# Feature-major output for token chunks 0 to 2 of a linear-attention and MLP block, with a new order of the first transfers

## The chip, the cores and the metric

The kernel runs on one core of a Trainium2 chip. The metric is device time in microseconds. Before the change the median of 13 runs is 205.41 us, the lowest 205.16, the highest 206.95. A profile is one execution taken by the hardware profiler; its span goes from the first to the last instruction, and its own device time is a little more than its span.

The engines are TensorE (PE; its weight loads PEld), VectorE (DVE), ScalarE (ACT), GpSimd (POOL) and SyncE (SP). SP here issues most transfers, in the order of its queue, and waits at each for what the transfer needs; ScalarE issues a few. The 16 DMA engines move the data.

## The reference

For x of 2048 tokens and 640 features (bf16), with 32 heads of 20 features and an MLP of 1536:

```python
xn = _layernorm(x, axis=-1)
return x + _A_ref(xn, A_wqkv, A_wo) + _B_ref(xn, B_w1, B_b1, B_w2, B_b2)
# _A_ref: linear attention
phi = lambda t: jnp.where(t > 0, t + 1, jnp.exp(t)) + 1e-6
pq, pk = phi(q), phi(k)
kv = jnp.einsum("bhsd,bhse->bhde", pk, v)
z = jnp.einsum("bhsd->bhd", pk)
o = einsum("bhqd,bhde->bhqe", pq, kv) / (einsum("bhqd,bhd->bhq", pq, z)[..., None] + 1e-6)
# ... then o @ wo
# _B_ref: gelu(x @ w1 + b1) @ w2 + b2
```

## The kernel before

Tokens are cut into 16 tiles of 128 (NT) and 4 chunks of 512 (NC). Features are 5 blocks of 128 (DT), MLP features 12 blocks (JT). A small planner records every instruction on its engine's list in the order of the program text and works out the semaphore waits from what each reads and writes. So each engine's order is the program's order. PSUM's eight banks are handed out in a ring: `take(1)` gives the next bank, `take(2)` the next even pair.

The stages on TensorE, in order:

1. Start: some matmuls on zeros, then LayerNorm of token tiles 0 and 1, their transposes through TensorE (L352, L389), and the first products with W1 (`h_first`, L400). `h_first(0, ...)` does the first two of the five feature blocks for four output blocks (8 matmuls, needing W1's rows 0 to 255), then the other three (12 matmuls, needing rows 256 to 639), and has pieces of tile 1's transposes between.
2. H: `h_unit` (L368) makes GELU(xn W1 + b1), feature-major, into HG (features x tokens), in matmuls of up to 512 tokens. From tile 4 on, xn is turned to xnT by DMA transposes on SP (L473).
3. K: 160 matmuls (L508); the activation `phi` on ScalarE and VectorE writes phi(K) to PK, which lies in the buffer of x. VectorE then sums it over tokens (`token_sum`), and `z_step` turns that sum by two DMA transposes.
4. G: xn^T phi(K), 160 matmuls (L541).
5. Q: `q_chunk(c)` (L553) makes phi(Q), feature-major, into PQ, chunk by chunk; between the chunks `kvt_step` (L567) and `mt_block` (L585) make the matrix M = (masked K^T V) Wo, which five DMA transposes put into Msb (L593). `x_again` loads x a second time into its old buffer (L638).
6. Out: for every token tile, 24 matmuls of HG with W2 and 10 of PQ with Msb (L669), each with a 128x128 block of tokens as weights and 320 output features as moving columns: two PSUM banks a tile. `out_w2(t)` does the first 24, `out_fin(t, b)` the other 10, two tiles behind. VectorE then adds PSUM and x (x with b2 added before, `xb`, L642) to out_sb (L689), and SP stores it (L692). The last tile (`out_last`, L706) goes in three pieces.

Beside the out stage run the denominators of the attention, a chunk ahead: `den_part` (L599, L602; VectorE, five a chunk), `den_gather` (L613; DMA over partitions), `den_inv` (L618, L621; VectorE), `den_spread` (L627; DMA), and `rden_scale` (L633; VectorE), which multiplies PQ's five blocks of the chunk by 1/den and so must be done before that chunk's PQ matmuls. For chunks 1 to 3 gathers and spreads go half on SP and half on ScalarE.

The first transfers' issues, SP and ScalarE (`dma_x` L245, `dma_w` L249):

```python
dma_x(0, 1)
dma_w("scalar", b1tmp[:], B_b1.rearrange("(a p) -> a p", p=P), r_b1tmp)
dma_w("scalar", W1[:, 0:KA, 0:FW], w1v[:, 0:KA, 0:FW], r_W1A)
dma_x(1, 1)
dma_w("sync", W1[:, KA:DT, 0:FW], w1v[:, KA:DT, 0:FW], r_W1[0])
dma_w1(1)
dma_x(2, 1)
dma_w1(2)
```

W1 comes in three blocks of 512 columns (FW); the first in two parts, rows 0 to 255 (KA = 2) and 256 to 639. SP's queue so has x0, x1, rows 256 to 639, block 1, x2, block 2; ScalarE's has b1 and rows 0 to 255.

Of the kernel before, what the change touches and what calls it, by code (L numbers as in the profile page):

```python
# [5 lines left out]
ALU = AluOpType  # L6
ACT = mybir.ActivationFunctionType
P = 128
FP32 = mybir.dt.float32
# [103 lines left out]
def bass_parallel_sum__linear_attn_block__dense_activation_gelu__prompt_kernel(  # L113
# [4 lines left out]
    NT = S // P  # L118
# [19 lines left out]
    with contextlib.ExitStack() as es:  # L138
# [13 lines left out]
        GTb = W1f[:, 0:DT * D].rearrange("p (k d) -> p k d", k=DT)  # L152
        KVT = W1f[:, DT * D:DT * D + NG * GW].rearrange("p (g d) -> p g d", g=NG)
        MT = W1f[:, DT * D + NG * GW:DT * D + NG * GW + DT * D].rearrange("p (b d) -> p b d", b=DT)
        Wqkv = sb("Wqkv", [P, DT, 3 * D], BF16)
        W2 = sb("W2", [P, JT, D], BF16)
        Wo = sb("Wo", [P, NG, D], BF16)
# [3 lines left out]
        zhl = Mf[:, 2 * D:4 * D].rearrange("p (a d) -> p a d", a=2)  # L161
        b1tmp = sb("b1tmp", [JT, P], BF16)
        b1c = sb("b1c", [P, JT], FP32)
        b2bc = sb("b2bc", [P, D], BF16)
        ident = sb("ident", [P, P], BF16)
        maskKV = sb("maskKV", [P, GW], BF16)
# [25 lines left out]
        def take(n):  # L192
            b = ring[0]
            if n == 2 and b % 2:
                b += 1
            b %= 8
            ring[0] = (b + n) % 8
            return b

        def bank(b, lo=0, hi=512):  # L200
            return ps[:, b * 512 + lo: b * 512 + hi]
# [14 lines left out]
        r_W1 = [R_("W1_%d" % i) for i in range(NW1)]  # L216
        r_Wq, r_Wk, r_Wv, r_W2 = R_("Wq"), R_("Wk"), R_("Wv"), R_("W2")
        r_Wo = [R_("Wo%d" % i) for i in range(2)]
        r_b1tmp, r_b1c, r_b2 = R_("b1tmp"), R_("b1c"), R_("b2")
        r_ident, r_small, r_masks, r_warm = R_("ident"), R_("small"), R_("masks"), R_("warm")  # L220
        r_stats = [[R_("stats%d_%d" % (i, h)) for h in range(2)] for i in range(4)]
# [18 lines left out]
        xv = A_x.rearrange("b s d -> (b s) d")  # L240
        ov = out.rearrange("b s d -> (b s) d")

        def dma_x(t, n):
            src = xv[t * P:(t + n) * P, :].rearrange("(t p) d -> p t d", p=P)
            Pl.ins("sync", lambda e: e.dma_start(x_in[:, t:t + n, :], src),  # L245
                   writes=r_x[t:t + n], dma=True)

        def dma_w(eng, dst, src, res):
            Pl.ins(eng, lambda e: e.dma_start(dst, src), writes=[res], dma=True)  # L249
# [5 lines left out]
            dma_w(eng, W1[:, :, i * FW:(i + 1) * FW], w1v[:, :, i * FW:(i + 1) * FW], r_W1[i])  # L255
        KA = 2
        dma_x(0, 1)
        dma_w("scalar", b1tmp[:], B_b1.rearrange("(a p) -> a p", p=P), r_b1tmp)
        dma_w("scalar", W1[:, 0:KA, 0:FW], w1v[:, 0:KA, 0:FW], r_W1A)
        dma_x(1, 1)  # L260
        dma_w("sync", W1[:, KA:DT, 0:FW], w1v[:, KA:DT, 0:FW], r_W1[0])
        dma_w1(1)
        dma_x(2, 1)
        dma_w1(2)
# [219 lines left out]
        def phi(src, b, nb, dst, res_dst, extra_w):  # L484
# [3 lines left out]
            else:  # L488
# [10 lines left out]
                                                       op0=ALU.max, op1=ALU.add),  # L499
                   reads=br + [re], writes=[res_dst] + extra_w)  # L500

        ring_e = [0]
        for t in range(NT):
            b = take(2)
# [44 lines left out]
        def q_chunk(c, after=None):  # L549
            cc = slice(c * CW, (c + 1) * CW)  # L550
            for j in range(DT):
                b = take(1)
                Pl.ins("tensor", [(lambda e, k=k, j=j, b=b: e.matmul(  # L553
                    bank(b), Wqkv[:, k, j:D:DT], xnT[:, k, cc],
                    start=(k == 0), stop=(k == DT - 1))) for k in range(DT)],
                    reads=[r_Wq] + r_xnT[c * CH:(c + 1) * CH], writes=[B_[b]])
                phi(bank(b), b, 1, PQ[:, j, cc], r_PQ[c][j], [])
                if after:
                    after(j)
# [4 lines left out]
        def kvt_step():  # L564
            for gs in parts:
                b = take(1)
                Pl.ins("tensor", [(lambda e, k=k, i=i, b=b, g0=gs[0]: e.matmul(  # L567
                    bank(b, GW * (i - g0), GW * (i - g0) + gw[i])[0:GW, :],
                    Wqkv[:, k, 2 * D + ge[i]:2 * D + ge[i] + GW],
                    GTb[:, k, GW * i:GW * i + gw[i]], start=(k == 0), stop=(k == DT - 1)))  # L570
                    for i in gs for k in range(DT)], reads=[r_Wv] + r_GT, writes=[B_[b]])
                for lo, hi, w in ([(0, G1, GW)] if gs[0] == 0 else [(G1, NG - 1, GW), (NG - 1, NG, gw[-1])]):
                    n = hi - lo
                    src = bank(b, GW * (lo - gs[0]), GW * (lo - gs[0]) + n * w)[0:GW, :].rearrange("p (g d) -> p g d", g=n)
                    msk = maskKV[0:GW, GW * lo - ge[lo]:GW * lo - ge[lo] + w].unsqueeze(1).to_broadcast([GW, n, w])
                    Pl.ins(v, lambda e, lo=lo, hi=hi, w=w, src=src, msk=msk: e.tensor_tensor(
                        out=KVT[0:GW, lo:hi, 0:w], in0=src, in1=msk, op=ALU.mult),
                        reads=[B_[b], r_masks], writes=[r_KVT] + r_W1)
# [30 lines left out]
        def den_gather(c):  # L609
            for q in range(MH):  # L610
                dst = y4[c % 2][H * q:H * (q + 1)]
                src = yv[c % 2][:, SW * q:SW * (q + 1)]
                Pl.ins(dma_q(c, q), lambda e, dst=dst, src=src: e.dma_start(dst, src),  # L613
                       reads=[r_y[c % 2]], writes=[r_y4[c % 2][q]], dma=True)

        def den_inv(c):
            s = c % 2
            Pl.ins(v, lambda e: e.tensor_reduce(out=den_sb[:, s, :], in_=y4[c % 2].rearrange("p m s -> p s m"),  # L618
                                                axis=mybir.AxisListType.X, op=ALU.add),
                   reads=r_y4[c % 2], writes=[r_den[s]])  # L620
            Pl.ins(v, lambda e: e.reciprocal(rden[:, s, :], den_sb[:, s, :]), reads=[r_den[s]], writes=[r_rden[s]])  # L621
# [8 lines left out]
        def rden_scale(c):  # L630
            cc = slice(c * CW, (c + 1) * CW)
            for j in range(DT):
                Pl.ins(v, lambda e, j=j: e.tensor_tensor(out=PQ[:, j, cc], in0=PQ[:, j, cc], in1=rdv[c], op=ALU.mult),  # L633
                       reads=r_rdb[c] + [r_PQ[c][j]], writes=[r_PQ[c][j]])

        def x_again(c):
            src = xv[c * CW:(c + 1) * CW, :].rearrange("(t p) d -> p t d", p=P)
            Pl.ins("sync", lambda e: e.dma_start(x_res[:, c * CH:(c + 1) * CH, :], src),  # L638
                   writes=[r_xr[c]] + r_PK[c * CH:(c + 1) * CH], dma=True)

        def xb(t):
            Pl.ins(v, lambda e: e.tensor_tensor(out=x_res[:, t, :], in0=x_res[:, t, :], in1=b2bc[:], op=ALU.add),  # L642
                   reads=[r_xr[t // CH], r_b2], writes=[r_xb[t]])
# [2 lines left out]
            x_again(c)  # L646
        q_chunk(0)
        kvt_step()
        q_chunk(1)

        def mt_and_den(j):
# [5 lines left out]
        den_spread(0)  # L657

        stores = []
        out_l = sb("out_l", [P, D], BF16)  # L660
        r_outl = [R_("outl%d" % i) for i in range(3)]

        def mm_ops(t, i):
# [11 lines left out]
        def out_w2(t, lo=0, hi=JT, b=None):  # L675
            b = take(2) if b is None else b
            for i in range(lo, hi):
                Pl.ins("tensor", [mm(b, t, i, 0), mm(b, t, i, 1)], reads=mm_reads(t, i), writes=B_[b:b + 2],
                       mark=(i == JT - 1))
            return b  # L680

        def out_fin(t, b):
            s = t % 2
            for i in range(JT, JT + DT):
                Pl.ins("tensor", [mm(b, t, i, 0), mm(b, t, i, 1)], reads=mm_reads(t, i), writes=B_[b:b + 2],
                       mark=(i == JT + DT - 1))
            if t >= CH:
                xb(t)
            Pl.ins(v, lambda e: e.tensor_tensor(out=halves(out_sb[:, s, :]), in0=pair(b),  # L689
                                                in1=halves(x_res[:, t, :]), op=ALU.add),  # L690
                   reads=B_[b:b + 2] + [r_xb[t]], writes=[r_out[s]])
            stores.append(Pl.ins("sync", lambda e: e.dma_start(ov[t * P:(t + 1) * P, :], out_sb[:, s, :]),  # L692
                                 reads=[r_out[s]], dma=True))
# [21 lines left out]
        def den_parts(c, lo, hi):  # L715
            for j in range(lo, hi):
                den_part(c, j)

        bs = [out_w2(t) for t in range(4)]
        den_parts(1, 0, DT)  # L720
        den_gather(1)
        rden_scale(0)
        for t in range(CH):
            xb(t)
        den_inv(1)
        den_spread(1)
        den_parts(2, 0, 1)
        out_fin(0, bs[0])
        den_parts(2, 1, 2)
        out_fin(1, bs[1])  # L730
        rden_scale(1)
        for t in range(2, NT - 1):
            out_fin(t, bs[t])
            if t == 2:
                den_parts(2, 2, DT)
                den_gather(2)
            elif t == 4:
                den_inv(2)
                den_spread(2)
            elif t == 5:  # L740
                den_parts(3, 0, DT)
                den_gather(3)
            elif t == 6:
                rden_scale(2)
            elif t == 7:
                den_inv(3)
                den_spread(3)
            elif t == 9:
                rden_scale(3)
            if t + 2 < NT - 1:  # L750
                bs.append(out_w2(t + 2))
        out_last(NT - 1)

        for ev in stores[:-1]:
# [38 lines left out]
```

## Time and profile before

| What | Value |
|---|---|
| Median of 13 runs | 205.41 us |
| The profiled execution's own time | 205.81 us |
| Its span | 204.6 us |
| TensorE busy (share of the span) | 200.1 us (98%) |
| VectorE busy | 127.0 us (62%) |
| ScalarE busy | 73.6 us (36%) |
| Out stage on the chain, all but the last tile (L669) | 69.28 us |
| Last tile (L706) | 4.67 us |
| Granted TensorE clock | 1.000 |

The page follows the chain of work back from the last instruction; its shares by engine are PE 95%, DMA 3%, the rest under 1%. A group of instructions has its line, the engine, output and inputs, the count, then busy time and the mean of one in ns, then the idle time of the engine before them and who ended most of it. A matmul's mean duration of 299 ns for 320 columns is its time in the pipeline; how fast they follow each other is read from the chain: a stretch divided by the matmuls in it. The record lacks a few matmuls: 117 of H's last 120 are listed.

### The profile page before, as it was taken

The numbers are of one execution on the slowest core, as the hardware profiler recorded it, in microseconds if no ns is written. First come the engines' busy times: TensorE is split into PE (matmuls) and PEld (weight loads), VectorE is DVE, ScalarE is ACT, GpSimd is POOL, SyncE is SP. The second block draws the span as 40 slices with busy tenths as digits, with TensorE's granted clock in tenths as the row PEclk, the third lists the DMA queues.
The fourth block names the chain that finished last, engine by engine and source line by source line (L and its number), as shares of the span: only waits on it lengthen the run. The fifth ranks groups of instructions, "written<-read, shape, count | busy, mean of one in ns | idle before, by whom it ended". The sixth has DMA issues, their size and how long they took to land.

```text
span 204.6 us, 3762 instructions
## 1 busy us (share of the span) xinstructions
PE 200.1 (98%) x1490; PEld 138.5 (68%) x1497; DVE 127.0 (62%) x247; ACT 73.6 (36%) x141; POOL 14.5 (7%) x43
## 2 busy tenths in 40 slices
PE   7899999999999999999999999999999999999996
PEld 2699987444447777777766565677777777777775
DVE  3577777200005888999558899899965776362242
ACT  3489887666667455121134596200000000000000
POOL 3134343300000000000000000000000000000000
DMA  5992953599950000000188035111330221100112
GB/s 157 362 361 64 83 94 79 96 309 290 278 204 0 0 0 0 3 0 3 32 242 303 5 64 101 50 26 51 93 114 35 58 87 50 43 35 34 62 37 64
DMA packets 30698, 20.29 MB, mean 99 GB/s; under 512 B 16263, under 2 KB 30679, under 8 KB 30679
## 3 DMA queue, kind: packets, MB, share of 16 engines
q1 hardware_dynamic: 28654, 19.18, 34.0%
q10 hardware_dynamic: 2024, 0.86, 1.7%
q8 instruction: 12, 0.20, 0.4%
q14 instruction: 8, 0.06, 0.1%
HBM read 12.72 MB, written 2.62 MB: 75 GB/s over the span
## 4 chain that ended last, share of the span: by engine, by line
PE 95%; DMA 3%; SPq 0%; issue 0%; DVE 0%
PE ps L669 34%; PE ps L368 24%; PE ps L508 11%; PE ps L541 11%; PE ps L553 10%; DMA W<-in_B_w_dram 3%; PE ps L706 2%; PE ps L400 1%; PE ps L567 1%; PE ps L585 1%; SPq L245 0%; PE ps L352 0%; DVE out_l L709 0%; PE ps L389 0%
## 5 line engine op out<-in xcount | busy, mean ns | idle before, releaser
L669 PE MATMUL ps<-W,HG 128*128 128x320 bf16 x360 | 50.9, 299 | 0.0
L368 PE MATMUL ps<-xnT,W 128*128 128x256 bf16 (+2 forms) x382 | 50.4, 293 | 0.2
L368 PEld LDWEIGHTS ps<-xnT,W 128*128 128x128 bf16 x385 | 33.8, 98 | 15.9
L669 PEld LDWEIGHTS ps<-W,HG 128*128 128x128 bf16 x360 | 35.2, 98 | 13.8
L372 ACT ACTIVATE HG<-ps,b1c 128x256 bf16<-128x256 f32 (+2 forms) x77 | 38.0, 516 | 12.7 <-PE ps L368 10.3
L689 DVE TENSOR_TENSOR out_sb<-ps,xPK 128x640 bf16<-128x640 f32 x15 | 12.4, 824 | 23.8 <-PE ps L669 23.5
L553 PE MATMUL ps<-xnT,Wqkv 128*128 128x512 bf16 x96 | 22.2, 379 | 0.2
L669 PE MATMUL ps<-Msb,PQ 128*128 128x320 bf16 x150 | 22.3, 299 | 0.0
L508 PE MATMUL ps<-Wqkv,xnT 128*128 128x320 bf16 x160 | 21.9, 299 | 0.0
L541 PE MATMUL ps<-xPK,xn_tm 128*128 128x320 bf16 x160 | 21.9, 299 | 0.0
L496 DVE TENSOR_SCALAR ek<-ek 128x640 bf16<-128x640 bf16 x16 | 5.2, 325 | 26.0 <-ACT ek L495 24.8
L508 PEld LDWEIGHTS ps<-Wqkv,xnT 128*128 128x128 bf16 x160 | 15.7, 98 | 6.2
L541 PEld LDWEIGHTS ps<-xPK,xn_tm 128*128 128x128 bf16 x160 | 15.7, 98 | 6.1
L669 PEld LDWEIGHTS ps<-Msb,PQ 128*128 128x128 bf16 x150 | 14.7, 98 | 5.7
L553 PEld LDWEIGHTS ps<-xnT,Wqkv 128*128 128x128 bf16 x100 | 11.3, 118 | 8.5
L324 DVE BATCH_NORM_STATS2 stats<-xPK 128x6 f32<-128x320 bf16 x32 | 14.7, 470 | 2.8 <-DMA xPK<-in_A_x_dram 2.8
L495 ACT ACTIVATE xn_tm<-ps 128x512 bf16<-128x512 f32 x20 | 11.9, 597 | 9.4 <-PE ps L553 8.7
L498 DVE SCALAR_TENSOR_TENSOR PQ<-ps,xn_tm 128x512 bf16<-128x512 f32 x20 | 13.8, 692 | 2.1
L495 ACT ACTIVATE ek<-ps 128x640 bf16<-128x640 f32 x16 | 11.3, 704 | 9.2 <-PE ps L508 9.2
L498 DVE SCALAR_TENSOR_TENSOR xPK<-ps,ek 128x640 bf16<-128x640 f32 x16 | 13.2, 824 | 1.7
L602 DVE SCALAR_TENSOR_TENSOR xn_tm<-PQ,z_sb,xn_tm 128x512 f32<-128x512 bf16 x16 | 12.0, 748 | 0.4
L528 DVE TENSOR_TENSOR Msb<-Msb,xPK 128x640 f32<-128x640 f32 x14 | 11.6, 825 | 0.5
(58 smaller groups left out, 110.5 us busy)
## 6 DMA issues: line engine op xcount, KB each, us to landing
xPK<-in_A_x_dram SPq DMA_DIRECT2D x6, 640.0 KB, 7.8
Wqkv<-in_A_wqkv_dram SPq DMA_DIRECT2D x3, 800.0 KB, 6.5
out_dram<-out_sb SPq DMA_DIRECT2D x15, 160.0 KB, 1.8
W<-in_B_w_dram SPq DMA_DIRECT2D x1, 1920.0 KB, 15.2
W<-in_B_w_dram SPq DMA_DIRECT2D x2, 640.0 KB, 7.8
Wo<-in_A_wo_dram SPq DMA_DIRECT2D x1, 750.0 KB, 11.8
xPK<-in_A_x_dram SPq DMA_DIRECT2D x4, 160.0 KB, 4.8
xPK<-in_A_x_dram SPq DMA_DIRECT2D x2, 320.0 KB, 7.7
```

The lines of the kernel that those rows point to most:

```text
L324: Pl.ins(v, lambda e: e.bn_stats(stats[:, s, 6 * h:6 * h + 6], x_in[:, t, h * HW:(h + 1) * HW]), reads=[r_x[t]], writes=[r_stats[s][h]])
L368: Pl.ins("tensor", [(lambda e, k=k: e.matmul(bank(b, 0, w), W1[:, k, jb * P:(jb + 1) * P], xnT[:, k, tok], start=(k == 0), stop=(k == DT - ...
L372: Pl.ins("scalar", lambda e: e.activation(HG[:, jb, tok], bank(b, 0, w), ACT.Gelu_apprx_tanh, bias=b1c[:, jb:jb + 1]), reads=[B_[b], r_b1c ...
L495: Pl.ins("scalar", lambda e: e.activation(e2, src, ACT.Exp), reads=br, writes=[re])
L498: Pl.ins(v, lambda e: e.scalar_tensor_tensor(out=d2, in0=src, scalar=0.0, in1=e2, op0=ALU.max, op1=ALU.add), reads=br + [re], writes=[res_ ...
L508: fns.append(lambda e, k=k, h=h, b=b, t=t: e.matmul(bank(b + h, 0, HW), xnT[:, k, t * P:(t + 1) * P], Wqkv[:, k, D + h * HW:D + (h + 1) * ...
L528: Pl.ins(v, lambda e, t=t: e.tensor_tensor(out=zsum, in0=zsum, in1=PK[:, t, :], op=ALU.add), reads=[r_PK[t], r_zsum], writes=[r_zsum])
L541: Pl.ins("tensor", [(lambda e, t=t, h=h, b=b, f=f: e.matmul(bank(b + h, 0, HW), xn_tm[:, t, f * P:(f + 1) * P], PK[:, t, h * HW:(h + 1) * ...
L553: Pl.ins("tensor", [(lambda e, k=k, j=j, b=b: e.matmul(bank(b), Wqkv[:, k, j:D:DT], xnT[:, k, cc], start=(k == 0), stop=(k == DT - 1))) fo ...
L602: Pl.ins(v, lambda e: e.scalar_tensor_tensor(out=yv[c % 2], in0=pq, scalar=z_sb[:, j:j + 1], in1=yv[c % 2], op0=ALU.mult, op1=ALU.add), re ...
L669: return lambda e: e.matmul(bank(b + h, 0, HW), l, r[:, h * HW:(h + 1) * HW], start=(i == 0), stop=(i == JT + DT - 1))
L689: Pl.ins(v, lambda e: e.tensor_tensor(out=halves(out_sb[:, s, :]), in0=pair(b), in1=halves(x_res[:, t, :]), op=ALU.add), reads=B_[b:b + 2] ...
```

## The change

In the out stage, chunks 0 to 2 (token tiles 0 to 11) are computed feature-major. A matmul now has a 128x128 block of W2 or Msb as weights and 512 tokens of HG or PQ as moving columns, and fills one bank with one feature block of one chunk. `fm` issues the 12 W2 matmuls of each of the five blocks first, then five PQ matmuls block by block. `fm_out` adds the bias (a column for each feature block, b2c) and x, feature-major, in one VectorE instruction, to a buffer oT that lies in W1's old place; SP then turns it back by a DMA transpose into x's buffer, and `fm_store` stores a whole chunk at once. For the residual, `x_turn` turns x of a chunk to feature-major by four DMA transposes into xnT, which is free by then: chunk 0 after `kvt_step`, chunk 1 after the gather of chunk 1, chunk 2 behind the first store. The bias column comes from a DMA transpose of b2 ahead of the K stage. Tiles 12 to 14 keep the old form, without a lookahead of two tiles; the last tile is unchanged.

In the start, x1 goes first on ScalarE's queue, W1's rows 0 to 255 move to SP behind x0, and rows 256 to 639 to ScalarE behind b1.

```diff
         dma_x(0, 1)
+        dma_x(1, 1, "scalar")
+        dma_w("sync", W1[:, 0:KA, 0:FW], w1v[:, 0:KA, 0:FW], r_W1A)
         dma_w("scalar", b1tmp[:], B_b1.rearrange("(a p) -> a p", p=P), r_b1tmp)
-        dma_w("scalar", W1[:, 0:KA, 0:FW], w1v[:, 0:KA, 0:FW], r_W1A)
-        dma_x(1, 1)
-        dma_w("sync", W1[:, KA:DT, 0:FW], w1v[:, KA:DT, 0:FW], r_W1[0])
+        dma_w("scalar", W1[:, KA:DT, 0:FW], w1v[:, KA:DT, 0:FW], r_W1[0])
         dma_w1(1)
...
+        Pl.ins("sync", lambda e: e.dma_start_transpose(b2T, b2bc[:]), reads=[r_b2], writes=[r_b2T], dma=True)
+        Pl.ins(v, lambda e: e.tensor_copy(b2c[:].unsqueeze(2), b2T[:, :, 0:1]), reads=[r_b2T], writes=[r_b2c])
...
+        def x_turn(c):
+            for t in range(c * CH, (c + 1) * CH):
+                Pl.ins("sync", lambda e, t=t: e.dma_start_transpose(xnT[:, :, t * P:(t + 1) * P], x_res[:, t, :]),
+                       reads=[r_xr[c]], writes=[r_xT[t], r_xnT[t]], dma=True)
...
         kvt_step()
+        x_turn(0)
         q_chunk(1)
...
-            if t >= CH:
-                xb(t)
+            xb(t)
...
+        def fm(c, nb, b, lo, hi):
+            cc = slice(c * CW, (c + 1) * CW)
+            ns = slice(nb * P, (nb + 1) * P)
+            for i in range(lo, hi):
+                l, r = (W2[:, i, ns], HG[:, i, cc]) if i < JT else (Msb[:, i - JT, ns], PQ[:, i - JT, cc])
...
+                Pl.ins("tensor", lambda e, l=l, r=r, i=i: e.matmul(bank(b), l, r, start=(i == 0), stop=(i == JT + DT - 1)),
+                       reads=rd, writes=[B_[b]], mark=(i == hi - 1))
+
+        def fm_out(c, nb, b):
...
+            Pl.ins(v, lambda e: e.scalar_tensor_tensor(out=oT[o], in0=bank(b), scalar=b2c[:, nb:nb + 1],
+                                                       in1=xnT[:, nb, cc], op0=ALU.add, op1=ALU.add),
...
+            Pl.ins("sync", lambda e: e.dma_start_transpose(x_res[:, c * CH:(c + 1) * CH, nb * P:(nb + 1) * P], oT[o]),
+                   reads=[r_oT[o]], writes=[r_omn[c][nb]], dma=True)
+
+        def fm_store(c):
+            dst = ov[c * CW:(c + 1) * CW, :].rearrange("(t p) d -> p t d", p=P)
+            stores.append(Pl.ins("sync", lambda e: e.dma_start(dst, x_res[:, c * CH:(c + 1) * CH, :]),
+                                 reads=r_omn[c], dma=True))
+
         den_parts(1, 0, DT)
         den_gather(1)
         rden_scale(0)
-        for t in range(CH):
-            xb(t)
+        x_turn(1)
         den_inv(1)
         den_spread(1)
...
+        for c in range(NF):
+            bs = [take(1) for nb in range(DT)]
+            for nb in range(DT):
+                fm(c, nb, bs[nb], 0, JT)
+            for nb in range(DT):
+                fm(c, nb, bs[nb], JT, JT + DT)
+                fm_out(c, nb, bs[nb])
+            if c + 2 < NC:
+                den_parts(c + 2, 0, DT)
+                den_gather(c + 2)
+            rden_scale(c + 1)
+            if c + 2 < NC:
+                den_inv(c + 2)
+                den_spread(c + 2)
+            fm_store(c)
+            if c == 0:
+                x_turn(2)
+        for t in range(NF * CH, NT - 1):
+            out_fin(t, out_w2(t))
         out_last(NT - 1)
```

More of the change, by code (lines that the diff above doesn't have):

```diff
@@ L154, in bass_parallel_sum__linear_attn_block__dense_activation_gelu__prompt_kernel @@
         MT = W1f[:, DT * D + NG * GW:DT * D + NG * GW + DT * D].rearrange("p (b d) -> p b d", b=DT)
+        oT = [W1f[:, CW * i:CW * (i + 1)] for i in range(2 * DT)]
+        out_l = sb("out_l", [P, D], BF16)
+        b2T = out_l[:].rearrange("p (k q) -> p k q", k=DT)
         Wqkv = sb("Wqkv", [P, DT, 3 * D], BF16)
@@ L163, in bass_parallel_sum__linear_attn_block__dense_activation_gelu__prompt_kernel @@
         b1c = sb("b1c", [P, JT], FP32)
+        b2c = sb("b2c", [P, DT], FP32)
         b2bc = sb("b2bc", [P, D], BF16)
@@ L218, in bass_parallel_sum__linear_attn_block__dense_activation_gelu__prompt_kernel @@
         r_Wo = [R_("Wo%d" % i) for i in range(2)]
+        r_oT = [R_("oT%d" % i) for i in range(2 * DT)]
+        r_omn = [[R_("om%d_%d" % (c, n)) for n in range(DT)] for c in range(NC)]
+        r_xT = [R_("xT%d" % t) for t in range(NT)]
+        r_b2T, r_b2c = R_("b2T"), R_("b2c")
         r_b1tmp, r_b1c, r_b2 = R_("b1tmp"), R_("b1c"), R_("b2")
@@ L241, in bass_parallel_sum__linear_attn_block__dense_activation_gelu__prompt_kernel, with dma_x @@
         ov = out.rearrange("b s d -> (b s) d")
-        def dma_x(t, n):
+        def dma_x(t, n, eng="sync"):
             src = xv[t * P:(t + n) * P, :].rearrange("(t p) d -> p t d", p=P)
-            Pl.ins("sync", lambda e: e.dma_start(x_in[:, t:t + n, :], src),
+            Pl.ins(eng, lambda e: e.dma_start(x_in[:, t:t + n, :], src),
                    writes=r_x[t:t + n], dma=True)
@@ L659, in bass_parallel_sum__linear_attn_block__dense_activation_gelu__prompt_kernel @@
         stores = []
-        out_l = sb("out_l", [P, D], BF16)
         r_outl = [R_("outl%d" % i) for i in range(3)]
@@ L717, in den_parts @@
                 den_part(c, j)
-        bs = [out_w2(t) for t in range(4)]
+        NF = NC - 1
+        def fm(c, nb, b, lo, hi):
[3 more added lines that the diff above has]
+                l, r = (W2[:, i, ns], HG[:, i, cc]) if i < JT else (Msb[:, i - JT, ns], PQ[:, i - JT, cc])
+                rd = ([r_W2] + [r_HG[t][i] for t in range(c * CH, (c + 1) * CH)] if i < JT
+                      else [r_M[nb], r_PQ[c][i - JT]])
+                Pl.ins("tensor", lambda e, l=l, r=r, i=i: e.matmul(bank(b), l, r, start=(i == 0), stop=(i == JT + DT - 1)),
+                       reads=rd, writes=[B_[b]], mark=(i == hi - 1))
+        def fm_out(c, nb, b):
+            o = (c % 2) * DT + nb
+            cc = slice(c * CW, (c + 1) * CW)
+            Pl.ins(v, lambda e: e.scalar_tensor_tensor(out=oT[o], in0=bank(b), scalar=b2c[:, nb:nb + 1],
+                                                       in1=xnT[:, nb, cc], op0=ALU.add, op1=ALU.add),
+                   reads=[B_[b], r_b2c] + r_xT[c * CH:(c + 1) * CH],
+                   writes=[r_oT[o]] + (r_GT + [r_KVT] + [r for m in r_MT for r in m] if c == 0 else []))
+            Pl.ins("sync", lambda e: e.dma_start_transpose(x_res[:, c * CH:(c + 1) * CH, nb * P:(nb + 1) * P], oT[o]),
[4 more added lines that the diff above has]
+                                 reads=r_omn[c], dma=True))
         den_parts(1, 0, DT)
@@ L722, in bass_parallel_sum__linear_attn_block__dense_activation_gelu__prompt_kernel @@
         rden_scale(0)
-        for t in range(CH):
-            xb(t)
+        x_turn(1)
         den_inv(1)
         den_spread(1)
[L727 to L751, printed above, removed]
+        for c in range(NF):
[17 more added lines that the diff above has]
+            out_fin(t, out_w2(t))
         out_last(NT - 1)
```

## The prediction, made before the run

> **What bounds the kernel now.** I read the page's busy shares first (PE 98%), then the chain of waits in order of time, then the timeline of the two stages that the diff touches, last the DMA queues. The chain:
>
> ```profile
> 1.73 5.82 DMA W<-in_B_w_dram
> 7.54 0.05 issue
> 7.59 0.51 PE ps L400 x6
> ...
> 34.75 10.74 PE ps L368 x49
> ...
> 60.59 21.73 PE ps L508 x160
> ...
> 128.78 69.28 PE ps L669 x510
> 198.05 4.67 PE ps L706 x51
> ```
>
> Each line is a start, a length and who holds the chain. From 7.59 us to 202.7 us it is TensorE without a break, so only two things change the time: how many TensorE microseconds the program contains, and when TensorE starts for good. The second hangs on one transfer, issued at 1.73 us, the rows 256 to 639 of W1's first column block. The timeline there (the bracket is the idle time before and who ended it):
>
> ```profile
> 6.46 0.61 PE L400 MATMUL ps<-xnT,W 128*128 128x128 bf16 x8
> 7.59 0.51 PE L400 MATMUL ps<-xnT,W 128*128 128x128 bf16 x6 [0.53 <-DMA W<-in_B_w_dram]
> 9.87 0.89 DVE L324 BATCH_NORM_STATS2 stats<-xPK 128x6 f32<-128x320 bf16 x2 [0.77 <-DMA xPK<-in_A_x_dram]
> ```
>
> The first eight matmuls need only W1's rows 0 to 255 and token tile 0; then TensorE idles 0.53 us. So at most 0.53 us can be won in the start without speeding up tile 0's LayerNorm too. The queues between 3 and 4 us (packets, MB, share) and the engines' windows:
>
> ```profile
> q10 hardware_dynamic: 129, 0.13, 65.1%
> q1 hardware_dynamic: 41, 0.04, 11.7%
> 3.00:4.00 1.00, 1.00 (x4) 0.16 (x2) 0.77 (x2) 0.43 (x2) 0.18 (x1) 1.00 0.77 167
> 4.00:5.00 1.00, 1.00 (x4) 0.30 (x4) 0.89 (x4) 0.18 (x1) 0.52 (x2) 1.00 0.97 292
> ```
>
> q10 is ScalarE's queue (rows 0 to 255), q1 SP's (rows 256 to 639). The last column is GB/s. The start is not at full rate: W1 ramps up from 167 through 292 to about 350 GB/s.
>
> The rest of what I price, from the page, the transposes' line and the timeline of the out stage:
>
> ```profile
> L689 DVE TENSOR_TENSOR out_sb<-ps,xPK 128x640 bf16<-128x640 f32 x15 | 12.4, 824 | 23.8 <-PE ps L669 23.5
> L498 DVE SCALAR_TENSOR_TENSOR PQ<-ps,xn_tm 128x512 bf16<-128x512 f32 x20 | 13.8, 692 | 2.1
> L602 DVE SCALAR_TENSOR_TENSOR xn_tm<-PQ,z_sb,xn_tm 128x512 f32<-128x512 bf16 x16 | 12.0, 748 | 0.4
> L473 SPq DMA_TRANSPOSE xnT<-xn_tm x12: 1199/1201/2065, 17.1 to 38.6; - x12
> DMA to landing us min/median/max: 2.6/2.6/4.9
> 118.92 6.73 SPq L593 DMA_TRANSPOSE Msb<-W  x5
> 126.36 2.64 SPq L613 DMA_DIRECT2D xn_tm<-xn_tm  x4
> 137.12 1.76 DVE L633 TENSOR_TENSOR PQ<-PQ,xn_tm 128x512 bf16<-128x512 bf16 x5
> 141.65 4.24 PE L669 MATMUL ps<-Msb,PQ 128*128 128x320 bf16 x30
> ```
>
> The first of these shows VectorE waiting for TensorE in the out stage, 23.5 us of it: VectorE has room there.
>
> [...] 69.28 us / 510 = 135.8 ns for 320 columns[...], and 34.70 to 60.59 us for the 120 matmuls of 512 columns, 215.8 ns[...]. [...] here a 98 ns load before each matmul lengthens neither pace. [...] The windows show both queues moving at once, but no case of two loaded queues sharing evenly. [...]
>
> **The change, part by part.**
>
> 1. Matmuls. Token tiles 0 to 11 took 12 x 34 = 408 matmuls of 320 columns: 408 x 0.1358 = 55.42 us. Now 3 chunks x 5 feature blocks x 17 = 255 of 512 columns: 255 x 0.2158 = 55.02 us. The columns are the same (130,560), so just 153 fixed costs go: **-0.40 us**, all on the chain. Tiles 12 to 15 keep their matmuls; that they lose their lookahead matters only if a wait appears (5).
>
> 2. Evacuation. Per chunk, 4 x 0.82 us (L689) and 4 x about 0.45 us (bias added to x) leave VectorE, and 5 additions of 128x512 out of PSUM come: between 0.692 (L498) and 0.748 us (L602, with a scalar column); I take 0.70. That is below the 5 x 0.216 = 1.08 us that TensorE spends on a block's last five matmuls, so VectorE keeps up. Cost 0, hidden by TensorE.
>
> 3. Banks. A chunk takes five; the next chunk's first three blocks go to the other three (7.8 us), by when the first was emptied. Cost 0.
>
> 4. SP's queue. Added: 1 transpose of b2, 12 of x and 15 of results; 1.20 us of SP each by L473 (the results' have four blocks instead of five, some 1.0 us), 2.6 us to landing. Each is followed in the queue. b2 lands near 50.6 us (issued at 41.6, 9.0 to landing); VectorE's copy behind it finishes near 54, inside its idle time of 24.8 us before 63.37. x of chunk 0 is turned once q_chunk(0) has read xnT, at 109.5: four issues to 114.5, before M's first transpose at 118.92, so M and the first denominator gather (126.36) don't move. x of chunk 1 is issued behind two gathers at 138.5 and holds SP to 143.5: den_spread(1) slips from 142.7 by 1 us, and its consumer now stands behind chunk 0's evacuation and five den_parts, about 151.5. No cost. x of chunk 2, behind the first store, ends near 163; it is needed after 178. The stores wait for the five result transposes and hold SP for some 3 us; behind them are the next chunk's result transposes, due 5 us later or more.
>
> 5. Scaled queries. Each chunk's attention matmuls come 60 x 0.216 = 12.95 us into it. Chunk 0: at 141.7; rden_scale(0) ends at 138.9 and nothing ahead of it changes. Chunk 1: due 160.1, scaled from 151.5 to 153.3. Chunk 2: due 178.4, done near 171.5 even with the gather, reduction and spread of chunk 2 (about 7 us) between. The tightest is tile 12: its W2 part takes 24 x 0.136 = 3.26 us; VectorE needs 0.70 for the last evacuation and 0.42 for the first scaled block, with a pause, about 1.2 us. **0**, with 2 us to spare.
>
> 6. Start. SP issues x0, W1 rows 0 to 255, then the second W1 block; ScalarE issues x1, b1, then rows 256 to 639. An issue takes ScalarE 0.66 us (b1, at 0.80) or 0.41, so the critical transfer is issued near 1.95, not 1.73. Rows 0 to 255 go from 1.50 to 1.26. x0 shares the engines with x1 and may come up to 0.4 us later (128 packets of x1 at full rate, as x1 trailed x0 by 0.37 us); the first eight matmuls then end at 7.47 instead of 7.07, still not above 7.54. The critical transfer is alone in its queue behind small ones, which may start it earlier; but the 640 KB block now runs beside it, no longer behind it. Of its 384 packets, between 128 and all 384 must be matched by packets of that block if turns are even: at 350 packets per us, +0.37 to +1.1 us. Against that stands the earlier start of W1 altogether, -0.24 us, and the 0.53 us that can be won if the transfer has its queue for itself. Bounds -0.5 to +1.1; I take **+0.1**, since the earlier start pays for most of the smallest loss. Nothing else hides it: TensorE moves with this landing one for one.
>
> Sum: -0.40 + 0.1 = -0.3 us on the profiled execution's own time of 205.81 (span 204.6 and 1.2 around it): 205.5. That execution lies 0.40 above the median of 205.41, so I forecast **205.1**.
>
> **The rivals.**
> - The start is won whole: rows 256 to 639 land before the eight matmuls end, -0.5. For: two queues are open early while engines stand half idle (167 GB/s). [...] 205.41 - 0.40 - 0.5 = 204.5.
> - The other side: even turns between the critical transfer and the 640 KB block. Place: W1 rows 256 to 639 on ScalarE's queue; price up to +1.1; it decides from a landing 0.8 us late (8.35) on. 205.41 - 0.40 + 1.1 = 206.1.
> - SP becomes the bound in the out stage: if a transpose there held SP or its landing grew to the 4.9 us seen once, M or den_gather(0) would slip. 2.8 us of slack at 141.65 speaks against; beyond it, 1 to 2 us: 206.5 to 207.
> - It doesn't do what it says: the 512-column matmuls do not run at 215.8 ns here, the fixed cost stays. H's stage with the same form speaks against. With the forecast's start: 205.5.
>
> **How the numbers follow.** 0.2% of 205.41 is 0.41 us, about what a measurement of this kernel can tell from no change. Forecast 0.58, own range 204.7 to 205.6: with the start within -0.3 to +0.6, 0.27 of it is faster and 0.31 the same. Start won whole 0.13, faster. Even turns 0.14: slower 0.12, same 0.02. SP 0.08, slower. Fixed cost stays 0.07, same. Together faster 0.40, same 0.40, slower 0.20. The range takes in both ends of the start, 204.5 to 206.1, and leaves out SP's case and part of the even turns, below 0.2.
>
> **What would show it.** Step 1: the out stage from its first matmul to the last tile's first, 69.28 before, 68.9 after, with no releaser but TensorE in the chain. Steps 2 to 5: no idle TensorE before a matmul of PQ. Step 6: the landing of W1's rows 256 to 639 against 7.54 us and the start of the ninth L400 matmul (its line moves). A wait on PQ or Msb, or VectorE in the chain before the end, would make the prediction wrong; so would a start outside -0.5 to +1.1.

## The result, and the profile after

The changed kernel takes 208.49 us (median of 11 runs, 207.08 to 210.24) against 205.51 us before (48 runs): a ratio of 1.0128, 95% interval 1.0109 to 1.0146. It is slower, outside the range of 204.5 to 206.1 us. The ratio leaves out the few executions in a slower state, and so is not the quotient of the two medians.

The chain of waits of the changed kernel, in order of time (start, length, who holds it; L408, L376, L743 and L685 are the old L400, L368 and the two forms of the output's matmuls):

```profile
1.95 7.76 DMA W<-in_B_w_dram
9.71 0.05 issue
9.76 0.82 PE ps L408 x6
...
10.79 0.64 PE ps L408 x6
...
13.34 2.73 PE ps L376 x25
...
132.11 9.71 PE ps L743 x45
...
185.04 2.11 PE ps L743 x9
187.15 13.86 PE ps L685 x102
201.01 4.67 PE ps L721 x51
```

The output stage did what was forecast. From 132.11 to 187.15 us it takes 55.04 us for 255 matmuls, and nothing but TensorE is in it; the 408 old ones took 69.28 x 408 / 510 = 55.42. The whole loss lies ahead of 13.34 us. Rows 256 to 639 of W1's first block land at 9.71 us, not 7.54. The timeline shows what TensorE did meanwhile:

```profile
6.96 0.61 PE L408 MATMUL ps<-xnT,W 128*128 128x128 bf16 x8
9.76 0.82 PE L408 MATMUL ps<-xnT,W 128*128 128x128 bf16 x6 [2.19 <-DMA W<-in_B_w_dram]
12.06 0.87 DVE L332 BATCH_NORM_STATS2 stats<-xPK 128x6 f32<-128x320 bf16 x2
```

An idle time of 0.53 us became 2.19. A second loss follows at once: six matmuls of 128 columns hold the chain for 0.64 us, 107 ns each, where before the same six took 0.34, 57 ns each. The windows name the reason (the number ahead of the last two is the granted TensorE clock):

```profile
8.00:9.00 1.00, 0.00 (x0) 0.00 (x0) 0.12 (x1) 0.00 (x0) 0.00 (x0) 1.00 1.05 360
9.00:10.00 1.00, 0.24 (x3) 0.25 (x4) 0.00 (x0) 0.00 (x0) 0.00 (x0) 0.60 1.09 389
10.00:11.00 1.00, 1.00 (x12) 1.00 (x10) 0.17 (x1) 0.69 (x2) 0.00 (x0) 0.50 1.08 385
11.00:12.00 1.00, 1.00 (x13) 1.00 (x11) 0.33 (x2) 0.69 (x2) 0.00 (x0) 0.50 1.07 359
12.00:13.00 1.00, 1.00 (x15) 1.00 (x14) 0.94 (x3) 0.12 (x1) 0.22 (x1) 0.69 1.07 362
```

From 9.2 us on, still in the idle time and 1.6 us after the end of the first eight matmuls (7.57 us), TensorE is granted half its clock (0.50) for 0.8 + 1 + 1 + 0.6 = 3.4 us.

The two profiled executions add up: TensorE resumes 2.17 us later (9.76 for 7.59), its work up to the 25 matmuls of 256 columns takes 3.58 us for 2.42 (+1.16), the output stage 0.38 less. Together +2.95; the spans differ by 207.5 - 204.6 = 2.9.

This is the account of one execution, of 208.81 us. Five executions of the changed kernel took only 207.1 to 207.9 us, the others 208.5 or more, and no trace of the five is kept. The late landing without the half clock would give 205.51 - 0.38 + 2.17 = 207.3 us: an estimate, from the median before and the two profiles above.

### The profile page after: what moved, and what is told of

Same layout as the page of the kernel before. It is cut to its first block, busy times and chain, and to the rows that moved or that the text cites. A ratio compares the mean times of both kernels' runs of the same rounds, so it can differ in the third digit from the quotient of the medians.

```text
span 207.5 us, 3474 instructions
## 1 busy us (share of the span) xinstructions
PE 200.9 (97%) x1332; PEld 124.8 (60%) x1344; DVE 124.3 (60%) x239; ACT 73.8 (36%) x141; POOL 14.4 (7%) x43
## 4 chain that ended last, share of the span: by engine, by line
PE 94%; DMA 4%; ACTq 1%; issue 0%; DVE 0%
PE ps L743 26%; PE ps L376 24%; PE ps L552 10%; PE ps L519 10%; PE ps L564 10%; PE ps L685 7%; DMA W<-in_B_w_dram 4%; PE ps L721 2%; PE ps L408 1%; PE ps L578 1%; PE ps L596 1%; ACTq L257 0%; PE ps L360 0%; PE ps L397 0%; ACTq L253 0%
## 5 line engine op out<-in xcount | busy, mean ns | idle before, releaser
L376 PE MATMUL ps<-xnT,W 128*128 128x256 bf16 (+2 forms) x382 | 50.4, 293 | 0.2
L376 PEld LDWEIGHTS ps<-xnT,W 128*128 128x128 bf16 x385 | 33.8, 98 | 15.9
L743 PE MATMUL ps<-HG,W 128*128 128x512 bf16 x177 | 39.2, 379 | 0.2
L743 PEld LDWEIGHTS ps<-HG,W 128*128 128x128 bf16 x180 | 17.6, 98 | 21.2
L749 DVE SCALAR_TENSOR_TENSOR W<-ps,b2c,xnT 128x512 bf16<-128x512 f32 x15 | 11.3, 751 | 8.8 <-PE ps L743 8.8
L743 PE MATMUL ps<-PQ,Msb 128*128 128x512 bf16 x73 | 16.4, 379 | 0.1
L743 PEld LDWEIGHTS ps<-PQ,Msb 128*128 128x128 bf16 x75 | 7.3, 98 | 8.8
```

The lines of the kernel that those rows point to most:

```text
L376: Pl.ins("tensor", [(lambda e, k=k: e.matmul(bank(b, 0, w), W1[:, k, jb * P:(jb + 1) * P], xnT[:, k, tok], start=(k == 0), stop=(k == DT - ...
L743: Pl.ins("tensor", lambda e, l=l, r=r, i=i: e.matmul(bank(b), l, r, start=(i == 0), stop=(i == JT + DT - 1)), reads=rd, writes=[B_[b]], ma ...
```

## The experiments

Three theories for the late landing: A, packets are handed to the DMA engines in the order of issue across both queues, and the rows are issued (1.95 us) just behind SP's 640 KB block 1 (1.73); B, the two queues share the engines in even turns, the forecast's rival; C, ScalarE's queue is slow for this transfer. Issue and landing (when the transfer is reported done) of the critical transfer (rows 256 to 639, unless said) in each profile:

| Kernel | Issued by, at | Block 1 issued | Landing | Median, us |
|---|---|---|---|---|
| before | SP, 1.73 | 2.19 | 7.54 | 205.51 |
| changed | ScalarE, 1.95 | 1.73 | 9.71 | 208.49 |
| changed, again | ScalarE, 1.95 | 1.73 | 10.04 | 209.37 |
| e1, output alone | SP, 1.75 | 2.22 | 6.54 | 205.23 |
| e2, start alone | ScalarE, 1.93 | 1.73 | 10.33 | 210.80 |
| e3, b1 to SP | ScalarE, 1.25 | 2.25 | 6.05 | 207.12 |
| e4, parts swapped | ScalarE, 1.50 | 2.21 | 6.14 | 205.23 |
| e5, no idle time | ScalarE, 1.94 | 1.73 | 10.38 | 209.50 |
| e5, again | ScalarE, 1.94 | 1.73 | 9.70 | 209.69 |
| e6, x2 ahead | ScalarE, 1.94 | 2.23 | 8.28 | 207.21 |
| e7, exchange (rows 0 to 255) | ScalarE, 1.94 | 1.73 | 10.39 | 211.41 (one run) |
| e8, block 1 held | ScalarE, 1.94 | after landing | 6.17 | 206.64 (one run) |
| e9, rows 0 to 255 first | SP, 1.73 | 2.20 | 5.94 | 206.33 |

One landing is one profile, and it varies: 6.54 and 7.54 us in the two kernels with the old start (before, e1), 9.70 to 10.38 in the five with the new one (changed twice, e2, e5 twice). In the experiments' comparisons the kernel before took 205.34 to 205.55 us.

**e1: the feature-major output alone**, with the old start.

```diff
-        dma_x(1, 1, "scalar")
-        dma_w("sync", W1[:, 0:KA, 0:FW], w1v[:, 0:KA, 0:FW], r_W1A)
         dma_w("scalar", b1tmp[:], B_b1.rearrange("(a p) -> a p", p=P), r_b1tmp)
-        dma_w("scalar", W1[:, KA:DT, 0:FW], w1v[:, KA:DT, 0:FW], r_W1[0])
+        dma_w("scalar", W1[:, 0:KA, 0:FW], w1v[:, 0:KA, 0:FW], r_W1A)
+        dma_x(1, 1)
+        dma_w("sync", W1[:, KA:DT, 0:FW], w1v[:, KA:DT, 0:FW], r_W1[0])
```

> The feature-major output with the old order of the first transfers. Theory (the whole loss is in the start, the output stage gains 0.40 us): ratio 0.998, 205.1 us, the chain from the first output matmul to tile 12's first 55.0 us, rows 256 to 639 of W1 landing near 7.5 us. Rival (the transposes in the output stage or the turned bias cost elsewhere too): 205.5 or more, with a wait other than TensorE in the chain after 8 us.

205.23 us against 205.49 in the same comparison, ratio 0.9984 (0.9973 to 0.9996). Its chain over the output stage:

```profile
128.62 55.04 PE ps L743 x255
183.65 13.86 PE ps L685 x102
197.51 4.67 PE ps L721 x51
```

One unbroken stretch of TensorE: the whole loss belongs to the start. The rows landed at 6.54 us, earlier than the 7.5 that was expected. This kernel is faster than both, by a little.

**e2: the new start alone**, with the old output stage: the start's lines of the change in the kernel before.

> The old output stage with the new order of the first transfers. Theory: rows 256 to 639 land between 9 and 10 us, TensorE resumes then and runs a few us at half clock in some executions; 207.5 to 209.3 us, 0.4 us above the changed kernel's. Rival (the start and the output stage act on each other): within 0.5 us of before.

210.80 us (4 runs), ratio 1.0229 (1.0179 to 1.0280). The landing, 10.33 us, is 0.3 later than expected and the time 1.5 us above the expected range: its profile, of the longest of the four runs, shows a mean granted clock of 0.984 (0.992 in the changed kernel's) and the slow pace for longer (the 25 matmuls of 256 columns take 3.65 us on the chain, 2.73 in the changed kernel). The rival is out: the start loses by itself.

**e3: b1 issued by SP**, so that the rows go ahead of block 1.

```diff
         dma_w("sync", W1[:, 0:KA, 0:FW], w1v[:, 0:KA, 0:FW], r_W1A)
-        dma_w("scalar", b1tmp[:], B_b1.rearrange("(a p) -> a p", p=P), r_b1tmp)
         dma_w("scalar", W1[:, KA:DT, 0:FW], w1v[:, KA:DT, 0:FW], r_W1[0])
+        dma_w("sync", b1tmp[:], B_b1.rearrange("(a p) -> a p", p=P), r_b1tmp)
         dma_w1(1)
```

> The changed kernel, but b1 is issued by SP behind rows 0 to 255, so that ScalarE issues rows 256 to 639 near 1.27 us, before SP's block 1 of W1 (near 2.4 us) instead of after it. Theory A (a transfer's packets are handed to the engines in the order of issue across both queues): the rows' packets start near 3 us, land by 7 us, time 204.6 to 205.2. Theory B (even turns with the 640 KB block): they start early but share; landing 8 to 8.8, 206 to 207. Theory C (ScalarE's queue is slow for this transfer whatever else is issued): landing 9 or later, 207.5 to 209.

The landing, 6.05 us, is theory A's; the time, 207.12 us and 1.0067 (1.0044 to 1.0091), is not. Another transfer took the place of the late one:

```profile
6.28 0.19 PE L324 MATMUL ps<-ident,b1tmp 12*128 12x12 bf16 x1 [2.29 <-DMA b1tmp<-in_B_b_dram]
```

b1 is 3 KB, issued at 1.73 us, behind the rows (1.25, on the other queue). TensorE waits for it until 6.28, just after the rows landed, with all LayerNorm transposes behind it, and then runs at half pace (14 matmuls with W1 take 1.49 us on the chain, 0.95 in e1). The queues between 4 and 5 us, of the changed kernel first:

```profile
q1 hardware_dynamic: 231, 0.23, 72.2%
q10 hardware_dynamic: 9, 0.01, 2.6%
```

and of e3:

```profile
q10 hardware_dynamic: 319, 0.32, 91.1%
q1 hardware_dynamic: 72, 0.05, 15.4%
```

The counts are packets, q10 is ScalarE's queue, q1 SP's. With even turns between two loaded queues q10 could not have 9 packets beside 231. In both the transfer issued first gets most of the packets at first, also across queues. It is not served whole before the other, as theory A in its strict form says: in the changed kernel block 1 was issued first and landed last, at 9.90 us (1.73 + 8.2):

```profile
W<-in_B_w_dram SPq DMA_DIRECT2D x1, 640.0 KB, 8.2
W<-in_B_w_dram ACTq DMA_DIRECT2D x1, 384.0 KB, 7.8
```

The last number is the time from issue to landing.

**e4: the two parts of the first block swapped**, in the old order of the first transfers.

```diff
         dma_w("scalar", b1tmp[:], B_b1.rearrange("(a p) -> a p", p=P), r_b1tmp)
-        dma_w("scalar", W1[:, 0:KA, 0:FW], w1v[:, 0:KA, 0:FW], r_W1A)
+        dma_w("scalar", W1[:, KA:DT, 0:FW], w1v[:, KA:DT, 0:FW], r_W1[0])
         dma_x(1, 1)
-        dma_w("sync", W1[:, KA:DT, 0:FW], w1v[:, KA:DT, 0:FW], r_W1[0])
+        dma_w("sync", W1[:, 0:KA, 0:FW], w1v[:, 0:KA, 0:FW], r_W1A)
```

> The feature-major output; the old order of the first transfers, but with the two parts of W1's first block exchanged: ScalarE issues b1 and rows 256 to 639 (near 1.5 us), SP x0, x1, rows 0 to 255 (near 1.73), block 1. Theory A: the rows are handed out first and land by 6.5 us; TensorE no longer waits for them at 7.1; 204.5 to 205.1. Theory B: turns with rows 0 to 255 and then with block 1: 7.5 to 8.2, 205.0 to 205.8. Theory C: 9 or later, 207 to 209.

The rows land at 6.14 us on ScalarE's queue: theory C is out, and the landing is A's. The time, 205.23 us and 0.9994 (0.9980 to 1.0007), is just above A's range: now rows 0 to 255 land last (6.78), and nothing is won over e1.

**e6: x2 ahead of block 1**, the smallest edit that reverses the order of the two issues.

```diff
-        dma_w1(1)
         dma_x(2, 1)
+        dma_w1(1)
         dma_w1(2)
```

> The changed kernel with SP's x2 (160 KB) issued ahead of W1's block 1 (640 KB), so that block 1 is issued near 2.25 us, after ScalarE's rows 256 to 639 (1.95), not before them (1.73). Nothing else moves. Theory A (packets are handed to the engines in the order of issue): the rows start once x2 is handed out and land by 7.2 us, 204.9 to 205.5. Theory B (even turns between the two queues): block 1 still runs beside them: 8 us or later, 205.8 to 207.5.

8.28 us, and 207.21 us, 1.0106 (1.0080 to 1.0132): both lie in theory B's ranges, so the order of issue alone does not explain the landing. Its queues from 5 to 6 us:

```profile
q10 hardware_dynamic: 132, 0.13, 53.1%
q1 hardware_dynamic: 88, 0.09, 34.8%
```

In the changed kernel q10 had 60 packets in that window, here 132, and block 1 runs beside them (x2's 160 KB now stand ahead of the rows too). So the earlier place brings the transfer forward (8.28 us for 9.71), and beside block 1 it is still later than without it (6.17 in e8 below); neither theory holds alone.

**e7: the other part in the late place.**

```diff
-        dma_w("sync", W1[:, 0:KA, 0:FW], w1v[:, 0:KA, 0:FW], r_W1A)
+        dma_w("sync", W1[:, KA:DT, 0:FW], w1v[:, KA:DT, 0:FW], r_W1[0])
         dma_w("scalar", b1tmp[:], B_b1.rearrange("(a p) -> a p", p=P), r_b1tmp)
-        dma_w("scalar", W1[:, KA:DT, 0:FW], w1v[:, KA:DT, 0:FW], r_W1[0])
+        dma_w("scalar", W1[:, 0:KA, 0:FW], w1v[:, 0:KA, 0:FW], r_W1A)
```

> The changed kernel with the two parts of W1's first block exchanged: rows 256 to 639 go to SP (1.27 us), rows 0 to 255 to ScalarE behind x1 and b1 (near 1.95), again after block 1 (1.73). Theory A (the place in the order of issue makes the delay, whichever transfer has it): rows 256 to 639 land by 6 us, rows 0 to 255 after 8.5; TensorE waits before its first matmul with W1; 207.5 to 210. Theory B (turns): the 256 packets land near 7.5, 205.5 to 206.5.

```profile
1.94 8.45 DMA W<-in_B_w_dram
10.39 0.05 issue
10.43 1.67 PE ps L408 x14
```

That is its chain: rows 0 to 255, a third fewer bytes, land at 10.39 us in the place behind block 1, and the rows in the early place at 4.9. The place makes the delay. The time, 211.41 us in one run, is above what was expected: in this profile TensorE waits 3.23 us before all of its work with W1, and runs at half pace after it (its first 14 matmuls take 1.67 us on the chain, 0.95 in e1).

**e8: block 1 held back** until the rows have landed.

```diff
-        dma_w1(1)
+        Pl.ins("sync", lambda e: e.dma_start(W1[:, :, FW:2 * FW], w1v[:, :, FW:2 * FW]),
+               reads=[r_W1[0]], writes=[r_W1[1]], dma=True)
```

> The changed kernel with SP's block 1 of W1 and all behind it held until rows 256 to 639 have landed, so that nothing is issued or moved beside them after 1.95 us. Theory A and B together (order sets when their packets start, turns with block 1 how long they take): packets from 3.5 us, landing 6.0 to 6.7 us. Theory B alone refuted if the landing stays above 9. Later loads are late then, so the time itself may be anything from 206 to 212.

The rows land at 6.17 us from the same issue time as in the changed kernel. Queues between 4 and 5 us:

```profile
q10 hardware_dynamic: 213, 0.22, 82.7%
q1 hardware_dynamic: 5, 0.00, 0.5%
```

So block 1, with the transfers behind it in SP's queue, makes 3.5 us of the landing at 9.71 (9.71 - 6.17). The rows' own packets show how it divides (in ScalarE's queue only they have 1,024 bytes, 384 of them): in the changed kernel the first starts at 4.61 us and the last at 9.22, in e6 at 4.28 and 7.80, here at 3.68 and 5.79. So some 0.9 us are a later start and 2.5 are moving beside block 1. What holds the start back is not shown; the 16 engines were not full between 4 and 5 us in the changed kernel (72.2% + 2.6%). The time, 206.64 us in one run, is above before although the rows are no longer late: here too matmuls go at half pace (14 in 1.49 us on the chain).

**e5: no idle TensorE in the wait.** Nine matmuls on zeros after the first eight with W1; their result is not used.

```diff
             for (ks, res) in (((0, 1), resA), ((2, 3, 4), r_xnT[t])):
+                if t == 0 and res is not resA:
+                    Pl.ins("tensor", [lambda e: e.matmul(bank(bA), warm[:, 0:P], warm[:], start=True, stop=True)
+                                      for _ in range(9)], reads=[r_warm], writes=[B_[bA]])
```

> The changed kernel with nine more matmuls on zeros (512 columns, some 1.9 us, their result is not used) after the first eight with W1, so that TensorE is busy while it waits for rows 256 to 639. Theory (about 1.1 us of the profiled loss is TensorE at half clock after the wait): the granted clock is 1.000 in every execution, the stretch from the landing to the 25 matmuls of 256 columns 2.3 us instead of 3.6, median 207.2 to 207.8. Rival (the half clock has another cause or costs nothing in most executions): 208.2 or more.

209.50 us: in the rival's range. It ran again beside the changed kernel, on one chip:

> The changed kernel again, unaltered, on the chip of the three runs beside it. Theory: median 207.5 to 209.5, rows 256 to 639 landing between 9.5 and 10.5 us; the executions whose granted clock is below 1.000 are the longer ones. Rival (the first comparison was one chip's): within 1 us of before.

> The kernel with nine matmuls on zeros in the wait, unaltered, now beside the changed kernel on one chip. In its first profile the stretch after the landing fell to 2.4 us as expected, but TensorE then waited 0.8 us for the turned xn of tile 5. Theory 1 (half clock after the wait is a loss of about 1.1 us): 0.5 to 1.2 us below the changed kernel. Theory 2 (VectorE's LayerNorm of the later tiles is held up by the same wait and sets the end of this stage, so a full clock only moves the wait): within 0.5 us of it.

The changed kernel took 209.37 us there (ratio 1.0185, 1.0164 to 1.0207), the filled one 209.69 (1.0194, 1.0169 to 1.0220): no difference clear of noise. The first of these expectations holds: the two executions with a lowered mean clock took 209.43 and 210.07 us, the other two 209.17 and 209.31. From the filled kernel's chain, then from its timeline:

```profile
10.87 1.30 PE ps L411 x20
12.17 2.73 PE ps L376 x25
```

```profile
25.57 4.61 PE L376 MATMUL ps<-xnT,W 128*128 128x128 bf16 x48 [1.01 <-DMA xnT<-xn_tm]
```

Twenty matmuls take 1.30 us as before the change (in the changed kernel 1.59): the full pace is kept. TensorE waits for the rows 2.19 and 2.5 us in the changed kernel's two profiles, and in both the granted clock falls to 0.50 (in the second near 10.9 us, after TensorE has resumed at 10.09); it waits 1.0 and 0.3 us in the filled kernel's two. That the wait brings the clock down is my reading of these four profiles. But TensorE then stops 1.01 us for the turned xn of token tile 5. LayerNorm is not what is late there. Its work stands behind the late rows and comes later than before the change (VectorE takes up tile 2 at 12.06 us in the changed kernel, at 9.87 before), but the filled kernel's is ahead of the changed kernel's: SP issues tile 5's transpose at 21.15 us, not 22.33. It is the time to landing that differs, in the changed kernel and then in the filled one:

```profile
xnT<-xn_tm SPq DMA_TRANSPOSE x1, 2.6
xnT<-xn_tm SPq DMA_TRANSPOSE x1, 4.4
```

Before the change three of these twelve transposes need 4.5 to 4.9 us, in the changed kernel two, 4.3 and 4.5; tile 5's takes 2.6 us in both profiles, and 4.1 and 4.4 in the filled kernel's two. Why is not shown. So theory 2 named the right number and not the right cause. The half clock was real, but what it costs by itself stays open: what the full pace won here was lost again at one slow landing.

**e9: rows 0 to 255 ahead of b1**, in the old start, as a try for a better kernel.

```diff
-        dma_w("scalar", b1tmp[:], B_b1.rearrange("(a p) -> a p", p=P), r_b1tmp)
         dma_w("scalar", W1[:, 0:KA, 0:FW], w1v[:, 0:KA, 0:FW], r_W1A)
+        dma_w("scalar", b1tmp[:], B_b1.rearrange("(a p) -> a p", p=P), r_b1tmp)
```

> The feature-major output with the old order of the first transfers, but ScalarE issues rows 0 to 255 of W1 before b1. Everything critical is then issued before block 1, and rows 0 to 255 first of all. Theory: rows 0 to 255 land by 4.8 us, rows 256 to 639 by 7 us, TensorE starts with W1 at 6.4 to 7.0: 204.9 to 205.3, the same as or up to 0.3 us below the feature-major kernel with the old start. Rival (the 256 packets push x1 back, which VectorE needs before it normalizes tile 0): 205.4 to 206.

206.33 us, 1.0022 (1.0005 to 1.0039), above both expected ranges, with executions near 205.1 and near 206.6 and little between. The transfers land as expected (4.2 and 5.9 us), x1 at 4.9. TensorE's timeline:

```profile
4.70 0.19 PE L324 MATMUL ps<-ident,b1tmp 12*128 12x12 bf16 x1 [0.70 <-DMA b1tmp<-in_B_b_dram]
7.05 1.68 PE L408 MATMUL ps<-xnT,W 128*128 128x128 bf16 x14
```

Small b1 is late again, and the fourteen matmuls go at 107 ns each (1.49 us on the chain). The changed kernel has that pace (0.64 us for six) at a granted clock of 0.50. The windows print 1.00 there, but this trace holds no record of the granted clock at all, and 1.00 is what they print then; so it is with before, e3, e6 and e8. One profile, of the longer sort; that the shorter executions lack this slow stretch was not seen.

## Why the prediction was wrong

- Step 1 held: -0.40 forecast, 55.42 - 55.04 = 0.38 less in the trace, and 0.26 (205.49 - 205.23) between e1's medians; the interval of its ratio takes in -0.40. The "fixed cost" of a matmul is an estimate: the paces before, 135.8 ns for 320 columns and 215.8 for 512, give 0.42 ns a column and some 2.5 ns a matmul beside them.
- Steps 2, 3 and 5 held. VectorE's added instruction takes 751 ns instead of the 700 that I took; no TensorE wait for a bank, PQ or Msb appears.
- Step 4 held in its result. Two sizes were off: a result's transpose holds SP for 1.27 us, not 1.0, and b2's transpose needed 9.9 us to landing instead of 2.6, while the 1.9 MB load of W2 was under way. VectorE's copy of the bias came at 64.25 us, and its next work at 66.71: 2.3 us were left of a slack that I had put at 9.
- **Step 6 failed.** I wrote that the critical transfer is "alone in its queue behind small ones, which may start it earlier", and set bounds of -0.5 to +1.1 us and +0.1 as the value. I moved its issue from 1.73 to 1.95 us and priced only even turns, which no window of before shows, at an estimated 350 packets per us (361 moved there between 5 and 6 us). But block 1's issue moved from 2.19 to 1.73, ahead of it, and the critical transfer, behind it, started late and then shared with it: between 4 and 5 us, 9 packets of the critical transfer moved. Nor did the queues reach 350: the windows from 4 to 8 us show 240 to 317 packets of both queues together. The landing is 2.17 us later; e3, e4, e6, e7 and e8 show the place, not the queue, as the cause. The profile before had a sign of it: of the 41 packets between 3 and 4 us that I read as rows 256 to 639, only 9 have their 1,024 bytes, beside 129 of the queue whose transfer was issued 0.23 us earlier. My rival "even turns" named the right pair of transfers, and too small a part of the price.
- "TensorE moves with this landing one for one" failed as well. In the idle time of 2.19 us the granted clock fell to 0.50, +1.16 us in the profiled execution, a term that was missing from the sum. What it costs in other executions stays open: where the full pace was kept (e5), a slow transpose took as much.

With step 6 at its measured +2.17 and +1.16, the sum is 205.81 - 0.38 + 3.33 = 208.76 us, and the profiled execution took 208.81.

## What to carry to other kernels

When transfers are moved between queues, write all issues of both queues on one time line: a transfer that many wait for should be issued before a large one that can wait, whichever queue each uses (ahead of block 1 on ScalarE's queue the rows landed at 6.05 and 6.14 us in e3 and e4, behind it at 9.71); here the rows landed 3.5 us later behind and beside a large transfer than without it, and 0.2 us of issue order put them there. A load that TensorE waits for in the first microseconds can cost more than its lateness: in the profiled execution the clock fell in the wait (+1.16 us). Such edits are worth a run by themselves: here one of two edits won a quarter of a microsecond and the other lost three.

## What was not expected of the hardware

- A 3 KB transfer, issued 0.5 us after a 384 KB one on the other queue and behind a 256 KB one on its own, kept TensorE waiting until 6.28 us, just after the 384 KB had landed at 6.05 (e3): being small did not bring it past them.
- 640 KB beside 384 KB nearly doubled the latter's time from issue to landing, from 4.2 us (e8) to 7.8.
- A transpose of 160 KB took 9.9 us to landing while a load of 1.9 MB was under way, and held SP for 4.7 us instead of 1.2.
- In e8 TensorE holds the chain without a break from 6.10 us on, and yet its matmuls of 128 columns went at 107 ns until 9.6 us; in the changed kernel the first eight took 0.61 us near 7 us, as long as before the change (1.03 in e6). Why the full pace begins so late in e8 is open. A printed clock of 1.00 can mean that nothing was recorded (e9): in the first microseconds the pace tells more.
